# Four edits to a tuned attention-and-FFN gradient kernel: the last forward blocks turned by TensorE and the FFN's inputs loaded first, a gate product placed behind the evictions, the row-norm gradient partly on ACT, the tail's packing pinned

## The chip, the cores and the metric

The kernel runs on one core of one Trainium2 chip. The metric is device time in microseconds (us) from the first to the last instruction of the core, some 1.7 us more than the span that the profile shows. The executions of one kernel mostly lie within 0.7% of each other, so I quote medians and, for comparisons, the ratio of fast runs with its 95% interval. All runs of this study were in the fast state; single fast runs reached 3169 us before and 3139 us in some of the variants.

Some words: TensorE writes its products to PSUM banks, and an eviction is the copy by which VectorE (DVE) or ScalarE (ACT) takes a result out of such a bank and frees it. GpSimd (Pool) and SyncE (SP) issue the transfers here. A hole is a stretch in which TensorE stands still. The granted clock is the share of its full clock that TensorE got, and the DMA share is the mean busy share of the 16 DMA engines.

## The reference, cut to what matters

```python
# 2048 tokens of width 448; 16 heads of 256; segments of 32 tokens behind 8 memory rows (64 segments)
for s in range(n_seg):                       # the memory makes this loop sequential
    h = concat([mem, xs]);  q, k, v = h @ Wq, h @ Wk, h @ Wv
    o = (softmax(mask(q @ k.T * scale)) @ v) @ Wo
    mem = o[:, :M];  outs.append(o[:, M:])
h  = x + A(layernorm(x))                     # A is the loop above
h2 = h + (silu(n @ w_gate) * (n @ w_up)) @ w_down,   n = layernorm(h)
# returned: h2 and, by jax.vjp, the gradients of x, mem0, Wq, Wk, Wv, Wo, w_gate, w_up, w_down
```

So there are four stages: a forward chain of 64 dependent segments, the FFN forward and backward (8 passes of 256 tokens), a backward chain of 64 dependent segments, and a tail in which the weight gradients are large matrix products over stored blocks.

## The kernel before

Only the places that the change touches are shown. W, A and B are regions of on-chip memory, dr[...] are scratch tensors in DRAM; `tc.issue_after(x)` places an instruction behind `x` in the order of its own engine.

The gradient of the row norm, nearly all on DVE (32 calls: 16 in the FFN, 16 in the backward chain):

```python
def ln_bwd(k, outs, dxn_ap, xn_ap, rstd_col, t1, junk):
    nc.vector.reduce_sum(out=m1[:], in_=dxn_ap, axis=AX.X)
    nc.vector.tensor_tensor_reduce(out=junk, in0=dxn_ap, in1=xn_ap, ..., accum_out=m2[:])
    # ... m1s = m1 / D, m2s = -m2 / D on 128x1
    nc.vector.tensor_scalar(out=t1, in0=dxn_ap, scalar1=m1s[:], scalar2=None, op0=ALU.subtract)
    nc.vector.scalar_tensor_tensor(out=t1, in0=xn_ap, scalar=m2s[:], in1=t1, op0=ALU.mult, op1=ALU.add)
    for out_ap, resid_ap, c0, c1 in outs:
        nc.vector.scalar_tensor_tensor(out=out_ap, in0=t1[:, c0:c1], scalar=rstd_col, in1=resid_ap, op0=ALU.mult, op1=ALU.add)
```

The end of the forward chain: the last blocks are turned to token-major order by DMA transposes on SP, behind the FFN's weight loads (`k.fl.at(...)`):

```python
        if jm == 15:
            # ... projection of the memory rows (32 matmuls into px)
            if end:
                at = k.fl.at(3).ins              # the last weight loads
        if jm == 15:
            for hf in range(2):
                to_token_major(mblk, NT + s // 16, hf, at)   # DMA transpose, then a store to X_o
            # ... memory rows: another DMA transpose, a store to XN
        # ...
        if end:
            for hf in range(2):
                to_token_major(xblk, t, hf, at)
```

An FFN pass (gates, ups, then the chain of products for the backward half):

```python
        def up(ps, fs):
            nc.scalar.copy(out=u[:, :, fs, :], in_=ps)
            nc.vector.tensor_tensor(out=z[:, :, fs, :], in0=ps, in1=g[:, :, fs, :], op=ALU.mult)
        # ...
        proj(Wg_sb, hnT, gate)
        nc.gpsimd.tensor_scalar(out=t1, in0=sg, scalar1=-1.0, scalar2=1.0, op0=ALU.mult, op1=ALU.add)
        proj(Wu_sb, hnT, up)
        to_v = nc.vector.tensor_tensor(out=t1, in0=g, in1=t1, op=ALU.mult)    # waits for Pool
```

The tail packs memory rows (M_v and so on) and turns them on TensorE between weight gradients:

```python
            def pack(ld=ld_b[g % 2], pk=pk_b[g % 2]):
                with tc.issue_after(k.last_om.ins):
                    nc.vector.tensor_copy(out=pk[:, 0:8], in_=...)
                nc.scalar.copy(out=pk[:, 8:16], in_=...)
            def turn(x_t, pk=pk_b[g % 2]):
                # ... 16 transposes on TensorE, two evictions
```

Of the kernel before, what the change touches and what calls it, by code (L numbers as in the profile page):

```python
# [247 lines left out]
def ln_bwd(k, outs, dxn_ap, xn_ap, rstd_col, t1, junk):  # L248

    nc, smal, D = k.nc, k._small, k.D  # L250
    m1 = smal.tile([P, 1], FP32, name="lnb_m1")
    nc.vector.reduce_sum(out=m1[:], in_=dxn_ap, axis=AX.X)
    m2 = smal.tile([P, 1], FP32, name="lnb_m2")
    nc.vector.tensor_tensor_reduce(out=junk, in0=dxn_ap, in1=xn_ap, scale=1.0, scalar=0.0,
                                   op0=ALU.mult, op1=ALU.add, accum_out=m2[:])
    m1s = smal.tile([P, 1], FP32, name="lnb_m1s")
    nc.vector.tensor_scalar(out=m1s[:], in0=m1[:], scalar1=1.0 / D, scalar2=None, op0=ALU.mult)
    m2s = smal.tile([P, 1], FP32, name="lnb_m2s")
    nc.vector.tensor_scalar(out=m2s[:], in0=m2[:], scalar1=-1.0 / D, scalar2=None, op0=ALU.mult)
    nc.vector.tensor_scalar(out=t1, in0=dxn_ap, scalar1=m1s[:], scalar2=None, op0=ALU.subtract)  # L260
    nc.vector.scalar_tensor_tensor(out=t1, in0=xn_ap, scalar=m2s[:], in1=t1, op0=ALU.mult, op1=ALU.add)
    for out_ap, resid_ap, c0, c1 in outs:
        nc.vector.scalar_tensor_tensor(out=out_ap, in0=t1[:, c0:c1], scalar=rstd_col, in1=resid_ap, op0=ALU.mult, op1=ALU.add)


class _FFNLoads:
# [31 lines left out]
    def at(self, place):  # L298
        k, sync = self.k, self.k.nc.sync
        if place == 0:  # L300
            self.rows(self.Wg_sb, k.aps["B_w_gate"])
            self.rows(self.Wu_sb, k.aps["B_w_up"])
        elif place == 1:
            self.load_in(0, 0)
            self.load_in(1, 1)
        elif place == 2:
            self.turned_rows(self.WdT_sb, k.dr["Td"])
            sync.dma_start(out=self.Wd_sb, in_=k.aps["B_w_down"].rearrange("(c p) d -> p c d", p=P))
        else:
            sync.dma_start(out=self.WgT_sb, in_=k.dr["Tg"])  # L310
            return sync.dma_start(out=self.WuT_sb, in_=k.dr["Tu"])
# [47 lines left out]
def forward_chain(k: _K):  # L359
# [193 lines left out]
    def to_token_major(blk, t, hf, ins=None):  # L553
        ot = stg()
        with tc.issue_after(ins) if ins is not None else nullcontext():
            nc.sync.dma_start_transpose(out=ot.rearrange("p (a b) -> p a b", b=P),
                                        in_=blk[:, 16 * hf:16 * hf + 16, :].rearrange("p c n -> p (c n)"))
        save((dr["X_o"][t][:, hf * 2048:(hf + 1) * 2048], ot))
# [42 lines left out]
    for s in range(NSEG):  # L601
# [9 lines left out]
        with k.prio.crit():  # L611
# [85 lines left out]
            if end:  # L697
                k.fl.at(0)
                k.fl.at(1)
# [13 lines left out]
            if end:  # L713
                k.fl.at(2)
# [46 lines left out]
        if r == 2:  # L761
            w = bu // 4
# [3 lines left out]
        at = None  # L766
        if jm == 15:
# [6 lines left out]
            if end:  # L774
                at = k.fl.at(3).ins
        if jm == 15:
            for hf in range(2):
                to_token_major(mblk, NT + s // 16, hf, at)
# [3 lines left out]
            r0 = (NT + s // 16) * P  # L782
# [3 lines left out]
        if end:  # L786
            for hf in range(2):
                to_token_major(xblk, t, hf, at)
# [7 lines left out]
def ffn_phase(k: _K, back):  # L796
# [36 lines left out]
    nc.gpsimd.dma_start(out=hc[:, 0:24, :], in_=xn[:, 8:32, :])  # L833
    nc.gpsimd.dma_start(out=hc[:, 24:32, :], in_=dr["XN"][S:, :].rearrange("(s m) d -> s m d", m=8))
    nc.gpsimd.dma_start(out=dr["HC"][S:, :].rearrange("(s m) d -> s m d", m=8), in_=xn[:, 0:8, :])
# [78 lines left out]
    for n, gi in enumerate(turns):  # L914
# [21 lines left out]
        def up(ps, fs):  # L936
            nc.scalar.copy(out=u[:, :, fs, :], in_=ps)
            nc.vector.tensor_tensor(out=z[:, :, fs, :], in0=ps, in1=g[:, :, fs, :], op=ALU.mult)
# [4 lines left out]
        nc.gpsimd.tensor_scalar(out=t1, in0=sg, scalar1=-1.0, scalar2=1.0, op0=ALU.mult, op1=ALU.add)  # L943
        proj(Wu_sb, hnT, up)
        to_v = nc.vector.tensor_tensor(out=t1, in0=g, in1=t1, op=ALU.mult)
# [61 lines left out]
def backward_chain(k: _K):  # L1007
# [38 lines left out]
    def load_seg(s):  # L1046
# [9 lines left out]
        nc.gpsimd.dma_start(out=P_sb.rearrange("p h n -> p (h n)"), in_=dr["P_all"][s])  # L1056
# [206 lines left out]
def tail_phase(k: _K):  # L1263
# [26 lines left out]

    def load_x(nm, hf):
# [11 lines left out]
    def load_m(nm, hf):  # L1303
        todo = []
        for g in range(NG):
# [4 lines left out]
            def pack(ld=ld_b[g % 2], pk=pk_b[g % 2]):  # L1310
                with tc.issue_after(k.last_om.ins):
                    nc.vector.tensor_copy(out=pk[:, 0:8], in_=ld[:, :, 0:8, :].rearrange("p s c m -> p c s m"))
                nc.scalar.copy(out=pk[:, 8:16], in_=ld[:, :, 8:16, :].rearrange("p s c m -> p c s m"))

            def turn(x_t, pk=pk_b[g % 2]):
                for q in range(2):
                    pt = k.ph1()
                    for i in range(8):
                        nc.tensor.transpose(pt[:, i * P:(i + 1) * P], pk[:, 8 * q + i].rearrange("p s m -> p (s m)"), ident[:, :])
# [10 lines left out]
    def d_by_e(lhs_of, rhs_of, nblk, widths, store, at=None):  # L1330

        pa = accs(7)
        for b0 in range(0, nblk, 4):
# [8 lines left out]
            for b in range(b0, min(nblk, b0 + 4)):  # L1342
                for g in range(2):
                    w = widths[g]
                    nc.tensor.matmul(pa[6][64 * g:64 * g + 64, 0:w], lhsT=lhs_of(b)[:, (KC - 1) * P:D], rhs=rhs_of(b, g),  # L1345
                                     start=(b == 0), stop=(b == nblk - 1), skip_group_check=True)
        for i in range(6):
            kc, g = divmod(i, 2)
            res = resbuf()
            k.evac(res[:, 0:widths[g]], pa[i][:, 0:widths[g]])  # L1350
            store(kc, g, res[:, 0:widths[g]])
        res = resbuf()
        for g in range(2):
            k.evac(res[64 * g:64 * g + 64, 0:widths[g]], pa[6][64 * g:64 * g + 64, 0:widths[g]])
            store(KC - 1, g, res[64 * g:64 * g + 64, 0:widths[g]])

    def rows_by_d(lhs_of, rhs_of, nblk, n, store):
        pa = accs(n)
        for bi, b in enumerate(nblk):
            for i in range(n):  # L1360
                nc.tensor.matmul(pa[i][:, 0:D], lhsT=lhs_of(b, i), rhs=rhs_of(b), start=(bi == 0), stop=(bi == len(nblk) - 1))  # L1361
        for i in range(n):
            res = resbuf()
            k.evac(res[:, 0:D], pa[i][:, 0:D])
# [116 lines left out]
```

## Time and profile before

| | us |
|---|---|
| median of 4 runs | 3152.92 (3142.21 to 3165.51) |
| profiled run, span and granted clock | 3151.8, 0.982 |
| forward chain, to its last DVE operation on the memory | 1051.6 |
| seam, from there to the first FFN projection | 14.0 |
| FFN, to the first matmul of the backward chain | 334.5 |
| from there to the score-gradient product of segment 63 | 5.9 |
| backward chain, that product of segment 63 to that of segment 0 | 1041.7 |
| tail, from there to the end | 704.1 |

I cut every profile of this study into the same stages by the start times of the same instructions, so a gain can be told by stage. The page and the waits for the first three stages stand in the prediction below. Two lines that it tells but does not show are TensorE's waits in the tail, from the view of waits (engine, tile and line, releaser: total us, times, longest):

```profile
PE ph L1319 <- DVE arA L1312: 13.3, 1, 13.3
PE psf L1361 <- DMA arA<-in_grad_out_dram: 4.5, 1, 4.5
```

L1319 is the first transpose of the packed memory rows; it stands ahead of the first weight gradient and waits for a packing copy.

### The profile page before, as it was taken

How to read it: one execution, taken by the hardware profiler on the slowest of the kernel's cores; microseconds unless marked ns; L12 is line 12 of the kernel's file. 1: busy time of each engine (PE TensorE's matmuls, PEld its weight loads, DVE VectorE, ACT ScalarE, POOL GpSimd, SP SyncE). 2: the span in 40 equal slices, each digit the busy share in tenths (PEclk: the TensorE clock that was granted, in tenths of full speed). 3: DMA queues.
4: the chain of work that ended last, by engine and by line, in shares of the span. 5: the costliest groups of instructions: out<-in, count | busy, mean ns of one | idle time of the engine just before them, and what ended most of it. 6: DMA issues, size and time to landing. Idle time of an engine off the chain costs nothing.

```text
span 3151.8 us, 108174 instructions
## 1 busy us (share of the span) xinstructions
PE 2920.1 (93%) x47572; PEld 1737.8 (55%) x47582; DVE 1360.2 (43%) x3441; ACT 1069.0 (34%) x2533; POOL 671.9 (21%) x1515
## 2 busy tenths in 40 slices
PE   6999999999988869999999999999999899999998
PEld 3555555555544445556666666666666454444443
DVE  4555455455455557664454444454444201111110
ACT  2444344344444424333333333433334101111210
POOL 2222222222222222231112112122111111211111
PEclk9999999999999989999999999999999899999999
DMA  6666666656755987794545545555545899969941
GB/s 239 174 174 173 168 172 171 180 161 170 194 164 164 263 215 188 186 320 121 139 132 142 142 128 140 141 134 148 130 139 132 272 283 245 189 183 201 186 151 56
DMA packets 747947, 552.33 MB, mean 175 GB/s; under 512 B 608916, under 2 KB 643716, under 8 KB 745044
## 3 DMA queue, kind: packets, MB, share of 16 engines
q1 hardware_dynamic: 695668, 389.32, 50.8%
q0 software_dynamic: 51808, 156.09, 14.9%
q8 instruction: 373, 6.11, 0.8%
q14 instruction: 98, 0.80, 0.1%
HBM read 168.01 MB, written 234.23 MB: 128 GB/s over the span
## 4 chain that ended last, share of the span: by engine, by line
PE 72%; issue 7%; DVE 7%; DMA 7%; ACT 3%; POOL 2%; SPq 1%; ACTq 0%; POOLq 0%; DVEq 0%
PE psf L1340 8%; PE po L1174 7%; PE psf L1125 6%; PE psf L535 5%; PE psf L646 5%; PE po L691 4%; PE psf L1361 4%; PE psf L1102 4%; PE fx L1238 3%; PE psf L868 3%; PE fx L464 2%; DVE arA L75 2%; PE fx L1345 2%; PE psf L549 2%; PE psf L1196 2%
## 5 line engine op out<-in xcount | busy, mean ns | idle before, releaser
L75 DVE CAST arA<-psf 128x256 bf16<-128x256 f32 (+3 forms) x933 | 427.0, 480 | 799.5 <-PE psf L1340 258.9
L76 ACT CAST arA<-psf 128x96 bf16<-128x96 f32 (+5 forms) x915 | 352.4, 409 | 1048.1 <-PE psf L1340 256.5
L1174 PE MATMUL po<-arW,arA 128*32 128x448 bf16 x6144 | 346.2, 354 | 5.0 <-DMA arW<-Tq 3.3
L1340 PE MATMUL psf<-arW,arA 128*128 128x512 bf16 x980 | 246.9, 379 | 0.0
L1125 PEld LDWEIGHTS <-arW 128*128 128x128 bf16 x8192 | 214.8, 96 | 27.7 <-issue 27.7
L1340 PEld LDWEIGHTS <-arA 128*128 128x128 bf16 x1440 | 136.0, 98 | 165.0 <-issue 13.7
L1125 PE MATMUL psf<-arA,arW 128*128 128x40 bf16 x8192 | 218.5, 180 | 8.6 <-DVE arA L1200 5.1
L646 PE MATMUL psf<-arW,arA 128*64 128x512 bf16 x1536 | 219.3, 386 | 0.0
L1174 PEld LDWEIGHTS <-arA 128*32 128x32 bf16 x6144 | 151.6, 96 | 115.3 <-ACT arA L76 9.3
L535 PE MATMUL psf<-arW,arA 128*32 128x512 bf16 x3072 | 191.8, 382 | 12.6 <-DVE arA L733 12.6
L868 PE MATMUL psf<-arW 128*128 128x256 bf16 (+1 forms) x1288 | 154.2, 282 | 36.2 <-DVE arA L934 19.2
L76 ACT CAST arB<-psf 128x64 bf16<-128x64 f32 (+3 forms) x384 | 121.8, 318 | 151.1 <-PE psf L539 106.6
L868 PEld LDWEIGHTS <-arW 128*128 128x128 bf16 (+1 forms) x1344 | 105.6, 99 | 91.4 <-issue 78.0
L691 PE MATMUL po<-arW,arA 128*32 128x256 bf16 (+1 forms) x4096 | 145.9, 269 | 9.7 <-DVE arA L75 7.5
L1135 ACT COPY arA<-psf 128x1024 bf16<-128x1024 bf16 x128 | 123.4, 1015 | 4.1 <-PE psf L1134 2.2
L1102 PEld LDWEIGHTS <-arW 128*128 128x128 bf16 x2048 | 86.4, 99 | 62.7 <-issue 58.9
L535 PEld LDWEIGHTS <-arA 128*32 128x32 bf16 x3072 | 70.2, 96 | 89.0 <-DVE arA L733 18.2
L691 PEld LDWEIGHTS <-arA 128*32 128x32 bf16 x4096 | 96.9, 98 | 32.3 <-DVE arA L75 10.8
L464 PE MATMUL fx<-arA,arW 128*128 128x64 bf16 (+1 forms) x2048 | 84.1, 195 | 32.5 <-ACT arB L76 19.3
L76 ACT COPY arA<-psf 128x512 bf16<-128x512 bf16 (+2 forms) x138 | 80.3, 582 | 92.8 <-DVE arA L75 90.7
L1102 PE MATMUL psf<-arB,arW 128*128 128x80 bf16 x2048 | 96.8, 201 | 14.4 <-DVE arB L1155 4.3
L464 PEld LDWEIGHTS <-arW 128*128 128x128 bf16 (+1 forms) x2048 | 70.6, 98 | 54.8 <-issue 32.5
(283 smaller groups left out, 4606.6 us busy)
## 6 DMA issues: line engine op xcount, KB each, us to landing
arW<-T SPq DMA_DIRECT2D x256, 128.0 KB
X_o<-arA SPq DMA_DIRECT2D x33, 512.0 KB
T<-arA SPq DMA_DIRECT2D x64, 256.0 KB
X_v<-arA POOLq DMA_DIRECT2D x32, 512.0 KB, 6.5
X_k<-arA POOLq DMA_DIRECT2D x32, 512.0 KB, 3.9
X_q<-arA POOLq DMA_DIRECT2D x32, 512.0 KB, 3.3
out_dram<-arA POOLq DMA_DIRECT2D x90, 128.0 KB, 3.9
VG<-arA SPq DMA_DIRECT2D x64, 160.0 KB
```

The lines of the kernel that those rows point to most:

```text
L75: return nc.vector.tensor_copy(out=out, in_=in_)
L76: return nc.scalar.copy(out=out, in_=in_)
L464: nc.tensor.matmul(banks[w][:, i * 64:(i + 1) * 64], lhsT=lhsT, rhs=xr[lo:hi, kc, :], start=(kc == 0 and i == 0), stop=(kc == KC - 1), ski ...
L535: nc.tensor.matmul(banks[w][32 * q:32 * q + 32, :], lhsT=hT_roll[:, kc, sl, M:L], rhs=(Wq_sb, Wk_sb)[w][:, kc, col(q, b)], start=(kc == 0) ...
L646: nc.tensor.matmul(pV[b][64 * g:64 * g + 64, 0:512], lhsT=hT_flat[:, kc, sl * L:sl * L + 64], rhs=Wv_sb[:, kc, n * 512:(n + 1) * 512], sta ...
L691: nc.tensor.matmul(pO[32 * q:32 * q + 32, 0:w], lhsT=xblk[:, j, r * SEG:(r + 1) * SEG], rhs=Wo_sb[:, cj(j), 256 * dh:256 * dh + w], start= ...
L868: nc.tensor.matmul(ps[fp][:, f2 * 256:(f2 + 1) * 256], lhsT=Wt[lo:hi, kc, c * P:(c + 1) * P], rhs=xT[lo:hi, kc, :], start=(kc == 0 and f2 ...
L1102: nc.tensor.matmul(ps[b][:, i * 2 * L:(i + 1) * 2 * L], lhsT=lhs[:, at, :], rhs=rhs_bd[:, cl // 2, :, :].rearrange("p g n -> p (g n)"), st ...
L1125: nc.tensor.matmul(pss[b][:, jj * L:(jj + 1) * L], lhsT=WoT_sb[:, kc, c * P:(c + 1) * P], rhs=do_roll[:, kc, sl, :], start=(kc == 0), stop ...
L1174: nc.tensor.matmul(pH[32 * (j % 4):32 * (j % 4) + 32, 0:D], lhsT=blk[nm][:, j, r * SEG:(r + 1) * SEG], rhs=WT[:, cj(j), :], start=(nm == " ...
L1340: nc.tensor.matmul(pa[2 * kc + g][:, 0:w], lhsT=lhs_of(b)[:, kc * P:(kc + 1) * P], rhs=rhs_of(b, g), start=(b == 0), stop=(b == nblk - 1), ...
L1361: nc.tensor.matmul(pa[i][:, 0:D], lhsT=lhs_of(b, i), rhs=rhs_of(b), start=(bi == 0), stop=(bi == len(nblk) - 1))
```

## The change

Its intent, in the author's four parts, split as I use them below:

1. **Seam**: TensorE turns the last blocks (68 transposes) in place of five DMA transposes; h and grad_out are loaded ahead of the weights; the copies of rows to HC move from the start of the FFN to passes 3 and 4; a load of P_all leaves Pool's line; one earlier DMA transpose (T0k of the last group of segments) moves from segment 62 to 59.
2. **Product**: the product that waits for Pool is placed behind the evictions of the up projection.
3. **Norm**: two of the row-norm gradient's passes go from DVE to ACT.
4. **Tail**: packing and turning are pinned behind the first weight gradient.

```diff
-    nc.vector.reduce_sum(out=m1[:], in_=dxn_ap, axis=AX.X)
+    nc.scalar.activation(out=t1, in_=dxn_ap, func=ACT.Copy, accum_out=m1[:])
...
-    nc.vector.tensor_scalar(out=t1, in0=dxn_ap, scalar1=m1s[:], scalar2=None, op0=ALU.subtract)
-    nc.vector.scalar_tensor_tensor(out=t1, in0=xn_ap, scalar=m2s[:], in1=t1, op0=ALU.mult, op1=ALU.add)
+    nc.vector.scalar_tensor_tensor(out=t1, in0=xn_ap, scalar=m2s[:], in1=dxn_ap, op0=ALU.mult, op1=ALU.add)
+    nc.scalar.activation(out=t1, in_=t1, func=ACT.Identity, scale=rstd_col, bias=m1s[:])
     for out_ap, resid_ap, c0, c1 in outs:
-        nc.vector.scalar_tensor_tensor(out=out_ap, in0=t1[:, c0:c1], scalar=rstd_col, in1=resid_ap, op0=ALU.mult, op1=ALU.add)
+        nc.vector.tensor_tensor(out=out_ap, in0=t1[:, c0:c1], in1=resid_ap, op=ALU.add)
... (FFN loads: load_in(0, 0) now first, load_in(1, 1) last)
+    def turned_by_pe(blk, halves):
+        for q in range(4):
+            pt = k.ps1()[:].bitcast(BF16)
+            for i in range(8):
+                nc.tensor.transpose(pt[:, i * P:(i + 1) * P], blk[:, 8 * q + i, :], ident[:, :])
+            k.evac(halves[q // 2][:, (q % 2) * 1024:(q % 2 + 1) * 1024], pt, "vs"[q % 2])
...
-        if r == 2:
-            w = bu // 4
+        if bu == 2 or bu == (3 if bm == NSEG // 8 - 1 else 6):
+            w = int(bu > 2)
...
+        if end:
+            last_x = [stg(), stg()]
+            turned_by_pe(xblk, last_x)
... (the same for mblk and the memory rows, then four plain stores to X_o behind the weight loads)
-        if end:
-            for hf in range(2):
-                to_token_major(xblk, t, hf, at)
...
-    nc.gpsimd.dma_start(out=hc[:, 0:24, :], in_=xn[:, 8:32, :])
-    ... (two more copies to HC)
+    def rows_of_contexts(i):
+        with tc.issue_after(k.pool_op.ins):
+            ... (the same three copies, called in passes 3 and 4)
...
-            nc.vector.tensor_tensor(out=z[:, :, fs, :], in0=ps, in1=g[:, :, fs, :], op=ALU.mult)
+            k.last_up = nc.vector.tensor_tensor(out=z[:, :, fs, :], in0=ps, in1=g[:, :, fs, :], op=ALU.mult)
...
-        to_v = nc.vector.tensor_tensor(out=t1, in0=g, in1=t1, op=ALU.mult)
+        with tc.issue_after(k.last_up.ins):
+            to_v = nc.vector.tensor_tensor(out=t1, in0=g, in1=t1, op=ALU.mult)
...
-        nc.gpsimd.dma_start(out=P_sb.rearrange("p h n -> p (h n)"), in_=dr["P_all"][s])
+        with tc.issue_after(k.pool_op.ins) if s == NSEG - 1 else nullcontext():
+            nc.gpsimd.dma_start(out=P_sb.rearrange("p h n -> p (h n)"), in_=dr["P_all"][s])
...
             def pack(ld=ld_b[g % 2], pk=pk_b[g % 2]):
-                with tc.issue_after(k.last_om.ins):
+                with tc.issue_after(k.last_ev["v"].ins):
                     nc.vector.tensor_copy(...)
-                nc.scalar.copy(...)
+                with tc.issue_after(k.last_ev["s"].ins):
+                    nc.scalar.copy(...)
... (turn: each transpose placed behind the last matmul of the gradient before it)
```

## The prediction

> **What bounds the kernel now.** The page's first part, then the busy tenths and the table of windows, split the span into four stages: the forward chain (to 1051 us), the FFN forward and backward (1066 to 1400), the backward chain (to 2463) and the tail of weight gradients (to 3152).
>
> ```profile
> PE 2920.1 (93%) x47572; PEld 1737.8 (55%) x47582; DVE 1360.2 (43%) x3441; ACT 1069.0 (34%) x2533; POOL 671.9 (21%) x1515
> 1102.80:1126.60 23.80, 4.63 (x41) 3.11 (x40) 4.04 (x10) 3.23 (x6) 3.76 (x7) 0.67 1.06 256
> 1160.40:1203.50 43.10, 37.67 (x269) 22.62 (x268) 29.42 (x51) 17.38 (x30) 11.22 (x17) 0.92 0.75 177
> 1241.70:1279.30 37.60, 35.75 (x270) 21.88 (x269) 27.43 (x44) 14.63 (x27) 7.97 (x11) 1.00 0.77 193
> ```
>
> TensorE is the bound (93%; DVE 43%, ACT 34%). A change gains only where TensorE stands still, so I looked for the holes. The second row is the start of FFN pass 1: 4.63 us of matmuls in 23.8, clock 0.67, DMA share 1.06 (saturated). The third and fourth rows are passes 2 and 4: the same 269 or 270 matmuls take 43.1 and 37.6 us. TensorE's waits in the FFN, in the view of waits, come down to two, and the timeline of TensorE shows what follows:
>
> ```profile
> PE psf L868 <- DVE arA L934: 19.2, 1, 19.2
> PE psf L868 <- DVE arA L938: 16.3, 7, 5.4
> 1178.52 8.28 PE L868 MATMUL psf<-arW 128*128 128x256 bf16 x56 [5.43 <-DVE arA L938]
> 1218.60 6.36 PE L868 MATMUL psf<-arW 128*128 128x256 bf16 x56 [2.09 <-DVE arA L938]
> 1335.32 7.93 PE L868 MATMUL psf<-arW 128*128 128x256 bf16 x56 [3.65 <-DVE arA L938]
> ```
>
> After a hole of 3.65 or 5.43 us the next 56 matmuls also run slower (7.93, 8.28 us against 6.36). The chain that ended last tells where the 19.2 us come from, and where TensorE stands still at the two seams:
>
> ```profile
> 1048.54 6.23 issue
> 1055.80 7.92 PE fx L770 x32
> ...
> 1112.05 7.29 DMA arA<-arA
> 1120.64 5.04 DMA DH<-dh_t
> ...
> 2466.42 9.24 DMA arA<-M_v
> 2475.74 0.44 DVE arA L1312
> 2476.22 0.29 PE ph L1319
> ```
>
> Seam one: TensorE is idle 4.7 us before L770, because Pool holds a load of P_all (L1056, needed only 350 us later) in front of the small copy L752 that L770 needs. Pass 1's gates write over the stage buffers that the last DMA transposes (L556) still read; those sit behind each other on the sync queue and end near 1119. Seam two: DVE and ACT stand at the packing copies (L1312, L1313) from 2460 and 2464 on for a load of M_v, and TensorE behind them for 13.3 us.
>
> **What the Trainium skill says.** "TensorE: Matmul & The Clock Gate", What's actually happening: about 3.4 us of idleness halves the clock until some 3.4 us of work. The trace agrees in kind (6.36 against 7.93 and 8.28 us); a 2.41 us hole before 1294.35 was enough too. Same page, PE-mode transpose: a transpose was measured at about 275 ns. This trace decides otherwise for batches: 54 at L843 took 3.18 us, 59 ns each, and 16 at L909 took 1.06 us, 66 ns. "DMA: Bandwidth & Descriptors", DMA Transpose (X-bar), Constraints: a plain DMA transpose can be issued from SP or ACT only. In the trace all are on SP, in line with the loads, and L764 held that line 11.97 us. "ScalarE: Activation LUTs", What ACT_TABLE_LOAD costs: an ACTIVATE costs 186 ns plus 0.833 ns per element, and 93 ns more per pointer operand. For 448 elements that gives 0.56 us plain and 0.75 us with scale and bias. The trace has plain copies of 128x448 at 0.53 to 0.57 us.
>
> **The change, part by part.** I also read the order of instructions of both builds. TensorE's, DVE's and ACT's are the same up to the end of the forward chain's last segment, so nothing moves in the first 1050 us but an early Pool copy to HC, where TensorE waits for no such copy.
>
> (1) Seam one. The P_all load leaves Pool's line: 4.7 us of idleness go. In come 64 transposes of the last two blocks and 4 of the memory rows: 68 x 62 ns = 4.2 us of TensorE, with nine PSUM evictions at 0.69 (DVE) and 1.0 us (ACT). In the new order the evictions of one staging half come only after pass 0's seven gates, because that buffer still waits for its own store; two of five PSUM banks stay held, which I put at 1 us. h and grad_out now come ahead of most weights: before, DVE waited for h until 1057.7, but TensorE had L770 to do until 1063.7, so this is hidden. Sum: about 0.
>
> (2) The hole of 19.2 us. Five DMA transposes of blocks and rows, and L764, leave the sync queue near the FFN's weights, and a part of the HC copies leaves this stretch. Pass 1's gates now wait for four plain X_o stores (2 MB). Bytes issued from 1040 to those stores: about 11 MB of weights, 0.5 of h and grad_out, 1.5 of T1, VG and Tv, 2 of X_o, 15 MB; at the 279 to 285 GB/s that the windows show here that is 53 us, so about 1093. The gates start near 1103. So I expect the hole to close: 19.2 us, plus the slow restart (128 matmuls in 17.07 us against 14.5 at 113 ns): 2.6 us.
>
> (3) The seven holes of 16.3 us. DVE ran the product L945, which waits for Pool's L943, in front of four or five of the evictions L938. The new order has it after the last of the seven in every pass. Gone: 16.3 us, and the slow restarts at 1178, 1294 and 1335: 1.9 + 1.6 + 1.6 = 5.1 us. Pool's lateness itself (it waits for grad_out, 2.58 us) stays, now behind 11.7 us of TensorE work: 56 matmuls of L868 (6.4) and 28 of L963 (5.3). DVE needs 2.0 + 2.0 + 3 x 1.05 = 7.1 us there, so it fits if Pool is less than some 4 us late.
>
> (2) and (3) together: 19.2 + 2.6 + 16.3 + 5.1 = 43.2 us at most. The HC copies (2.5 MB) now come in passes 3 and 4: 5 and 4 us of a full DMA in passes of 36 us at a share of 0.8, so late loads there are likely. I take 7 us off: **36 us**.
>
> (4) The row-norm gradient. For each of 32 tiles DVE loses a reduction (0.62) and a subtraction (0.68), and its last operations turn into plain adds; ACT gains two passes, 0.56 + 0.75. DVE sheds some 40 us in all, but TensorE waits for it nowhere in these places: in the backward chain the segment after a norm has its first DVE eviction 0.2 us late and TensorE does not stop. DVE's sum of products now also waits for ACT's pass where they share a buffer. The new order has ACT's two passes between evictions in which ACT waited 1.2 and 1.6 us for TensorE, so they fit. **1 us.**
>
> (5) The tail. Packing and turning are pinned behind the first weight gradient; the 13.3 us of TensorE go, and a slow restart (120 matmuls in 24.7 us against 22.7): 15 us at most. But the X_o blocks that this gradient reads are issued by SP until 2484, each waiting for an earlier one to land, at a DMA share of 0.92 to 0.98, and a part of its other operand (L349) until 2490. If TensorE starts at 2467 it catches up with them: block 16 of 20 would be due at 2467 + 16 x 1.14 = 2485 and lands near 2491. So about 7 us are given back. **8 us.** From 2505 to 3092 TensorE is busy 99 to 100%: nothing to gain. The last 60 us (15 us idle, a load of grad_out that needs HC's place) are untouched.
>
> Sum: 0 + 36 + 1 + 8 = 45 us: 3158.8 - 45 = **3114 us**.
>
> **Rivals.** (a) A new wait takes the hole's place: the X_o stores stand behind all weights in the same queue, and if the DMA reaches them at 1115 instead of 1093, 12 us come back. For it: the DMA share was 1.08. Against it: the transposes and HC copies that made it so are gone. Time: about 3126. (b) The FFN becomes bound by DMA or by the Pool-DVE-ACT chain: 30.8 us of DMA per pass (0.8 x 38.5) in 36, and ACT's second norm pass stands between gates. A quarter of the gain would go: about 3125. (c) All holes close and the tail isn't paced by loads: 43 + 15 + 5 = 63 us: 3096. Against it: the DMA shares above. (d) The extra evictions and the held PSUM banks at seam one cost more than the wait they replace, 5 us or so: 3119.
>
> **Range and chances.** Three runs before spread from 3142 to 3166, so 12 us either way for the median. With (a) and (b) together I come to 3138, with (c) to 3096: range **3093 to 3138**. Faster by over 2% needs 63 us, which is (c) in full: **0.15**. Slower by over 2% needs a new stall of 100 us: **0.02**. Within 2%: **0.83**.
>
> **What would show it.** TensorE's waits for the up evictions (L938 before) should be near 0, and passes 2 to 6 take 36 to 37 us each at a clock near 1.0. No hole over 5 us at the start of pass 1; if it is there, its releaser is a store of X_o. TensorE's first FFN projection starts within 2 us of 1065.6. The backward chain still takes 16.04 us a segment and 16.9 after a norm. The tail's first gradient starts near 2467 on the old clock but shows small DMA waits. The prediction is wrong if the X_o stores end after 1110, if HC copies stall passes 3 and 4 by more than 5 us each, or if the backward chain's segments change.

## The result, and the profile after

The changed kernel took 3108.39 us (median of 4 runs, 3105.46 to 3112.69), the kernel before 3152.92. The ratio is 0.9858 with a 95% interval of 0.9816 to 0.9901. A ratio here is the mean time of one kernel's fast runs over that of the other's in the same rounds, so it is not quite the ratio of the medians. The gain is 44.5 us, 1.4%: within 2%, as predicted, and 5.6 us below the predicted 3114. The prediction started from 3158.8 us, the median of the three runs that it had.

| stage, us | before | after | difference |
|---|---|---|---|
| forward chain | 1051.6 | 1052.5 | +0.9 |
| seam | 14.0 | 12.4 | -1.6 |
| FFN | 334.5 | 293.5 | -41.0 |
| to segment 63 | 5.9 | 7.3 | +1.4 |
| backward chain | 1041.7 | 1034.0 | -7.7 |
| tail | 704.1 | 704.0 | -0.1 |

The busy times on the page of the changed kernel:

```profile
PE 2914.8 (94%) x47640; PEld 1735.5 (56%) x47650; DVE 1331.6 (43%) x3381; ACT 1112.6 (36%) x2634; POOL 674.7 (22%) x1511
```

Its table of windows for passes 1 to 4 (stretch, its length, then busy time with instructions of TensorE, weight loads, DVE, ACT and Pool, the granted clock, the DMA share and GB/s):

```profile
1101.80:1138.90 37.10, 35.43 (x268) 21.56 (x266) 27.05 (x46) 16.92 (x33) 11.22 (x17) 1.00 0.93 237
1138.90:1175.00 36.10, 36.10 (x272) 22.03 (x271) 26.95 (x47) 18.50 (x35) 10.32 (x15) 1.00 0.86 197
1175.00:1211.00 36.00, 36.00 (x270) 21.81 (x269) 25.40 (x40) 18.17 (x34) 8.45 (x12) 1.00 0.97 219
1211.00:1247.50 36.50, 35.66 (x269) 21.70 (x268) 25.34 (x40) 16.92 (x33) 8.96 (x13) 1.00 0.97 240
```

TensorE is as busy as before in total; it only stands still less. Pass 1, which began with 23.8 us of near standstill and took 57.6 us (1102.8 to 1160.4), is now a pass like the others, at a clock of 1.00. Passes 3 and 4, which carry the HC copies, have a DMA share of 0.97 and are hardly longer. TensorE's waits in the FFN of the changed kernel:

```profile
PE fx L1014 <- DVE arW L990: 2.5, 2, 1.7
...
PE psf L890 <- DVE arA L956: 0.7, 2, 0.4
```

And TensorE's timeline there (start, us, line, operation, tiles, shape, count; an idle time before it would stand in brackets):

```profile
1101.88 18.97 PE L890 MATMUL psf<-arW 128*128 128x256 bf16 x168
...
1139.40 18.97 PE L890 MATMUL psf<-arW 128*128 128x256 bf16 x168
...
1175.10 19.28 PE L890 MATMUL psf<-arW 128*128 128x256 bf16 x168
```

The waits of 19.2 and 16.3 us for DVE's evictions are gone. The 112 gate and up matmuls of a pass and the 56 of the data gradient behind them, which were two groups with a hole between them, run as one group of 168 in 18.97 us, 113 ns each. Pool's lateness itself stays, as predicted, but only DVE sees it now: the view of the product's line says what DVE waited for ahead of it (us, times), here before:

```profile
  POOL arW L943: 15.7, 6
```

And in the changed kernel:

```profile
  POOL arW L965: 9.5, 4
```

At the seam, TensorE's timeline of the changed kernel shows the new transposes (L557, L790) around the projection that used to wait 4.68 us for Pool:

```profile
1051.90 1.96 PE L557 MATMUL psf<-ident,arA 128*128 128x128 bf16 x32
1053.69 6.22 PE L778 MATMUL fx<-arW,arA 128*128 128x448 bf16 x32
1059.75 2.08 PE L557 MATMUL psf<-ident,arA 128*128 128x128 bf16 x32
1061.96 0.38 PE L790 MATMUL psf<-ident,arB 128*128 128x128 bf16 x4
```

The tail is the surprise. TensorE's waits there in the changed kernel:

```profile
PE psf L1396 <- DMA arW<-X_o: 13.0, 1, 13.0
PE psf L1396 <- DMA arA<-in_grad_out_dram: 3.3, 1, 3.3
```

And the chain of waits ahead of its first weight gradient (start, us, what):

```profile
2417.27 13.43 DMA arW<-X_o
2430.74 2.05 PE psf L1396 x5
```

The 13.3 us wait for a packing copy has turned into a 13.0 us wait for the first X_o load. The first matmul of the first weight gradient comes 31.0 us after segment 0's product, against 31.9 before, where the whole of 15 us at most was to be gained. The backward chain is 7.7 us shorter, which no step of the prediction had.

### The profile page after: what moved, and what is told of

Same layout as the page of the kernel before. It is cut to its first block, busy times and chain, and to the rows that moved or that the text cites. A ratio compares the mean times of both kernels' runs of the same rounds, so it can differ in the third digit from the quotient of the medians.

```text
span 3103.7 us, 108341 instructions
## 1 busy us (share of the span) xinstructions
PE 2914.8 (94%) x47640; PEld 1735.5 (56%) x47650; DVE 1331.6 (43%) x3381; ACT 1112.6 (36%) x2634; POOL 674.7 (22%) x1511
## 4 chain that ended last, share of the span: by engine, by line
PE 72%; issue 11%; DVE 6%; DMA 5%; ACT 4%; POOL 2%; SPq 1%; ACTq 0%; POOLq 0%; DVEq 0%
PE po L1200 7%; PE psf L1151 7%; PE psf L535 6%; PE psf L652 5%; PE po L697 4%; PE psf L1375 4%; PE psf L890 4%; PE psf L1128 4%; PE psf L1396 4%; PE fx L1264 3%; PE fx L1014 3%; PE fx L464 2%; PE psf L1222 2%; DVE arA L75 2%; PE psf L549 2%
## 5 line engine op out<-in xcount | busy, mean ns | idle before, releaser
L75 DVE CAST arA<-psf 128x256 bf16<-128x256 f32 (+3 forms) x933 | 427.2, 480 | 808.6 <-PE psf L1375 275.2
L535 PE MATMUL psf<-arW,arA 128*32 128x512 bf16 x3072 | 193.8, 385 | 12.5 <-DVE arA L738 12.5
L890 PE MATMUL psf<-arW 128*128 128x256 bf16 (+1 forms) x1288 | 146.3, 274 | 1.3 <-DVE arA L956 0.7
L890 PEld LDWEIGHTS <-arW 128*128 128x128 bf16 (+1 forms) x1344 | 102.4, 97 | 51.4 <-issue 40.8
L76 ACT COPY arA<-psf 128x512 bf16<-128x512 bf16 (+3 forms) x142 | 84.3, 594 | 99.9 <-DVE arA L75 90.3
L464 PE MATMUL fx<-arA,arW 128*128 128x64 bf16 (+1 forms) x2048 | 84.3, 196 | 32.4 <-ACT arB L76 19.2
L1436 POOL DMA_DIRECT2D out_dram<-arA x96 | 51.7, 546 | 249.7 <-DVE arA L75 246.9
```

Of the source, the lines that this page charges most:

```text
L75: return nc.vector.tensor_copy(out=out, in_=in_)
L76: return nc.scalar.copy(out=out, in_=in_)
L464: nc.tensor.matmul(banks[w][:, i * 64:(i + 1) * 64], lhsT=lhsT, rhs=xr[lo:hi, kc, :], start=(kc == 0 and i == 0), stop=(kc == KC - 1), ski ...
L535: nc.tensor.matmul(banks[w][32 * q:32 * q + 32, :], lhsT=hT_roll[:, kc, sl, M:L], rhs=(Wq_sb, Wk_sb)[w][:, kc, col(q, b)], start=(kc == 0) ...
L890: nc.tensor.matmul(ps[fp][:, f2 * 256:(f2 + 1) * 256], lhsT=Wt[lo:hi, kc, c * P:(c + 1) * P], rhs=xT[lo:hi, kc, :], start=(kc == 0 and f2 ...
```

## The experiments

Three questions were open. Which part brought the 41 us of the FFN, and do the parts add up? Did the norm on ACT shorten the backward chain? Why did the tail gain nothing? My theory for the three: product and seam bring the FFN's gain and nearly add up; the backward chain's 7.7 us are chance; the tail is paced by the X_o loads. The rivals: the norm has a share in both chains, and the packing pin works but something else in the changed kernel takes its gain back.

### 1. Each part alone on the kernel before (one call, 3 rounds each)

**The product alone** (before, plus `k.last_up = ...` in `up` and):

```diff
-        to_v = nc.vector.tensor_tensor(out=t1, in0=g, in1=t1, op=ALU.mult)
+        with tc.issue_after(k.last_up.ins):
+            to_v = nc.vector.tensor_tensor(out=t1, in0=g, in1=t1, op=ALU.mult)
```

> The kernel before with part (3) alone: the gate product g*t1 is placed behind the last up eviction of its pass. Theory A (the seven holes of 16.3 us and their slow restarts of 5.1 us are this one misplaced product): waits of TensorE for the up evictions fall from 16.3 us to under 2 us, FFN stage (first gate matmul to first matmul of the backward chain, 334.5 us before) falls by 19 to 22 us, while the 19.2 us hole at the start of pass 1 stays. Rival (the holes come from Pool and DMA being late, so they only move on to the next place that needs the product): FFN stage falls by less than 8 us and TensorE's waits move to the matmuls of the data gradient. Whole time about 3132 under A, about 3147 under the rival.

Measured: 3134.37 us (3131.47 to 3138.2), ratio to before 0.9925 [0.9901, 0.9949]. The FFN took 313.0 us, 21.5 less. TensorE's waits in the FFN:

```profile
PE psf L868 <- DVE arA L934: 19.3, 1, 19.3
```

The hole of pass 1 is as before, and the waits for the up evictions are gone from the list; they have not moved to another place either. Passes 2 to 5 started at 1168.98, 1204.67, 1240.68 and 1276.38, so they take 35.7 to 36.0 us each. One reordered DVE instruction per pass is half of the whole gain, and 21.5 is what the prediction's part (3) says (16.3 + 5.1 = 21.4).

**The norm alone** (before, with `ln_bwd` of the changed kernel):

> The kernel before with part (4) alone: the row-norm gradient partly on ACT. Between the two profiles the backward chain (first product of segment 63 to that of segment 0) fell from 1041.7 to 1034.0 us. Theory A (the norm is not the cause; the 7.7 us are mostly single late segments that differ from run to run): segments after a norm fall by 0.07 us each (16.92 to 16.85), about 1 us in all, and the sum of the late segments stays a matter of chance; FFN within 1 us of 334.5. Rival (the norm on DVE held up the evictions): the backward chain again takes about 1034 us with the same few late segments as the changed kernel. Whole time within 3 us of before under A, 8 us less under the rival.

Measured: 3149.23 us (3147.85 to 3154.92), ratio 0.9975 [0.9951, 0.9999]. The segments after a norm took 16.86 us in the median against 16.91, so the chain gains 16 x 0.05 = 0.8 us. The backward chain as a whole was 1035.7 us here, but it was 1035.7 with the product alone too, where nothing in it differs from before. The FFN was 329.4 us, 5.1 less than before. I had not expected this; the waits for the up evictions were 13.7 instead of 16.3 us and pass 1's hole 18.4 instead of 19.2. With a single profile, and a spread of 5.0 us among FFNs of equal instructions (below), it may be chance. The interval of the times just excludes 1, though, so whether the norm alone gains a few us stays open.

What the moved passes cost, by groups of instructions (busy us, mean ns, then the idle time before them) in the backward chain of the kernel before:

```profile
L260 DVE TENSOR_SCALAR t<-fx,lnb_m1s 128x448 f32<-128x448 f32 x15 | 10.2, 680 | 0.0
...
L252 DVE TENSOR_REDUCE lnb_m<-fx 128x1 f32<-128x448 f32 x16 | 10.0, 625 | 18.6 <-PE fx L1253 18.6
```

And in that of the changed kernel:

```profile
L261 ACT ACTIVATE t<-t,lnb_m1s,rstd 128x448 f32<-128x448 f32 x16 | 12.2, 761 | 20.9 <-DVE t L260 19.7
...
L252 ACT ACTIVATE t<-fx 128x448 f32<-128x448 f32 x16 | 9.0, 562 | 0.7 <-PE fx L1279 0.7
```

DVE loses 0.62 and 0.68 us a call and ACT gains 0.56 and 0.76, as the prediction's estimate had it, and 0.21 more for a read of the accumulator, which it had not. TensorE waits for neither.

**The tail alone** (before, with `tail_phase` of the changed kernel):

> The kernel before with part (5) alone: packing and turning in the tail pinned. In the changed kernel the 13.3 us wait for the packing was followed by a 13.0 us wait for the first X_o block, and the tail took 704.0 against 704.1 us. Theory A (the DMA engines are full from the end of the backward chain on, so the wait only changes its name): the tail takes 703 to 705 us, the wait for packing is gone and one of 11 to 14 us for X_o is there. Rival (the wait for X_o comes from another part of the change, such as the shifted loads): the tail falls to 695 to 697 us. Whole time the same as before under A, 8 us less under the rival.

Measured: 3148.73 us (3145.47 to 3153.76), ratio 0.9971 [0.9947, 0.9996]. The tail took 696.3 us, 7.8 less than before; the prediction had 8 for it. TensorE's first wait in it:

```profile
PE psf L1370 <- DMA arW<-X_o: 7.1, 1, 7.1
```

So the pin does what it was meant to do on its own, and the X_o loads hold TensorE for 7.1 us, not 13. The wait stands in front of the first block (first matmul at 2472.51), and no later block waits. The rival held: in the changed kernel something else makes these loads land later.

**The seam alone** (the changed kernel with the norm, the tail and the place of the product as before):

> The kernel before with parts (1) and (2) alone: last blocks turned by TensorE, h and grad_out ahead of weights, HC copies and P_all load later; norm, product and tail as before. Theory A (parts add up): the 19.2 us hole at pass 1 is gone, FFN stage falls from 334.5 by 20 to 23 us, the holes for the up evictions stay at 14 to 18 us; the seam itself (end of the last output projection to the first gate matmul) stays within 2 us of 14.4 us. Rival (holes hide each other): with pass 1 unblocked the up-eviction holes grow, FFN falls by less than 15 us. Whole time about 3130 under A, above 3137 under the rival.

Measured: 3135.79 us (3132.14 to 3136.92), ratio 0.9925 [0.9898, 0.9952]. The seam took 12.5 us, 1.5 less, but the FFN 325.6: only 8.9 less, although the hole of pass 1 is closed. TensorE's waits in the FFN:

```profile
PE psf L890 <- DVE arA L960: 24.5, 8, 6.7
```

The 56 data-gradient matmuls of pass 1, behind the up evictions, in TensorE's timeline:

```profile
1123.17 8.50 PE L890 MATMUL psf<-arW 128*128 128x256 bf16 x56 [6.65 <-DVE arA L960]
```

The waits for the up evictions grew from 16.3 to 24.5 us: pass 1 now has one too (6.65 us, with a slow restart). Closing one hole lets TensorE run into the next wait earlier: the rival held. Alone, product, seam and norm gain 21.5 + 8.9 + 5.1 = 35.5 us in the FFN; together they gain 41.0. They are not independent: the product's new place takes away the wait into which the seam's gain ran. And the tail of this kernel, with the old packing, shows that the seam part is enough to hold the X_o loads back: its first X_o load was issued 17.2 us after the first of the DCt loads ahead of it in SP's line, as in the changed kernel (17.0), against 12.4 before and 12.1 with the tail alone. Over all profiles it is 11.3 to 13.5 us in the four without the seam part and 15.0 to 17.8 in the nine with it and an unchanged order of these loads.

### 2. The changed kernel again, and parts taken out of it (one call, 3 rounds each)

**Unchanged, once more:**

> The changed kernel once more, unchanged. Theory S (systematic): the late start of the X_o loads follows from the order in which Pool's transfers were issued, so the tail is again 703 to 705.5 us and TensorE again waits 12 to 14 us for the first X_o block. Theory C (chance): the loads landed late only in that profile, and the tail comes out near 696 (the value of the tail part alone), the time near 3101. On the backward chain: if its 1034 us are chance it may come out anywhere from 1033 to 1042; if the seam part causes it, within 1033 to 1036.

Measured: 3109.37 us (3105.83 to 3112.01), ratio 0.986 [0.984, 0.9879]. Tail 704.1 us with a wait of 13.0 us for X_o: the same as before to 0.1 us, so the late loads are systematic. The backward chain, however, was 1039.5 instead of 1034.0 us with the same instructions, and the forward chain 1047.6 instead of 1052.5.

**With the tail of the kernel before:**

> The changed kernel with the tail's packing and turning in the order of before. Theory S (in the combination the pin gains nothing, because TensorE only exchanges a wait for packing against a wait for X_o loads): tail 703 to 706 us, TensorE waits 15 to 18 us for a packing copy on DVE and little for X_o; ratio to the changed kernel within 0.1%, so about 3109. Rival (the pin is worth its 7.8 us here too): tail 711 to 713, time about 3117.

Measured: 3114.6 us (3111.64 to 3135.75), ratio 0.9892 [0.9854, 0.9929]. Tail 704.8 us. TensorE waits as before, and a little longer:

```profile
PE ph L1345 <- DVE arA L1338: 15.8, 1, 15.8
```

In this company the pin gains 0.7 us in the tail (704.8 against 704.1): with it TensorE waits for X_o, without it for the packing copy, until about the same time. The medians differ by 5 us, so the expected 0.1% was missed. In this profile 2 to 5 us of it lie in the FFN (298.5 us, with a wait of 4.3 us in pass 0), but the other three runs have no profile, so that the pin is worth a few us here is not ruled out.

**With the first M_v fetches placed behind the first weight gradient** (they read many small pieces just when the X_o loads are under way):

```diff
-    mems[0][0][0]()
+    with tc.issue_after(k.first_dwo.ins):
+        mems[0][0][0]()
```

> The changed kernel with the first two M_v fetches (many small pieces, on Pool's queue) held back until the first weight gradient's last matmul. Theory D (the DMA engines are full at this seam, and the M_v pieces take the bandwidth from the X_o loads): the first X_o block lands 6 to 9 us earlier, TensorE's wait for it falls from 13.0 to 4 to 7 us, tail 695 to 698, time about 3101. Rival E (the X_o loads are late because the loads of DCt before them on the same queue are late): wait for X_o stays 12 to 14 us, tail 702 to 705. Rival F (packing now comes too late): a new wait of 5 us or more for the packing or turning behind the first gradient, tail 704 or more.

Measured: 3112.98 us (3104.61 to 3119.1), ratio 0.987 [0.9842, 0.9899]. This run tested nothing. The edit ties a Pool transfer to a matmul, but `issue_after` only orders instructions of one engine, and the order of instructions turned out the same as in the changed kernel on every engine, wait for wait. I should have compared the orders before the run. It serves as a third profile of the changed kernel: FFN 294.1, backward chain 1043.2, tail 711.8 (with another 6.8 us wait of a TensorE transpose for an eviction, which came up at 4.7 us in one later run and at 2 us or less in the others), forward chain 1048.5. Three profiles of the same instructions thus span 9.2 us in the backward chain.

**With the DMA transposes of the last blocks** (`forward_chain` of the kernel before, which also puts the transpose of T0k back to segment 62; the new order of loads and all else as changed):

> The changed kernel with the last blocks of the forward chain turned by DMA transposes again, all else kept (h and grad_out first, row copies late, product last). Theory T (the transposes on the sync queue made the hole at the start of pass 1): TensorE waits 12 to 19 us at the start of pass 1, FFN 306 to 313 us, time 3121 to 3128; the seam is up to 5 us shorter or longer. Rival H (the row copies in this stretch made it): no hole over 5 us, FFN 292 to 297, time within 4 us of the changed kernel.

Measured: 3126.33 us (3118.55 to 3133.33), ratio 0.9906 [0.9881, 0.9931]. FFN 324.5 us. TensorE's timeline in pass 1:

```profile
1131.39 18.42 PE L872 MATMUL psf<-arW 128*128 128x256 bf16 x128 [23.12 <-DVE arA L938]
```

Two rows of SP's timeline ahead of it:

```profile
1054.32 19.22 SPq L763 DMA_TRANSPOSE arA<-arA  x1
...
1083.94 14.07 SPq L556 DMA_TRANSPOSE arA<-arA  x2
```

The hole is back, at 23.1 us. Followed back in the chain of waits it ends in the transposes and their stores: TensorE waits for DVE's gate evictions, those for the staging buffer, and that for a DMA transpose of 9.36 us and the X_o store behind it. Theory T held, and the FFN was even longer than its 306 to 313 (the profiled run was the slowest of the four, 3133.33 us). The first row above is the transpose of T0k, so this run does not tell its share from that of the last blocks. Nor are the 19.22 us the cost of a transpose alone: in the changed kernel a plain store in the same place, behind the same weight loads, held SP's line for 11.23 us. The seam was 8.0 us here: the loads' new order and the moved P_all load save 14.0 - 8.0 = 6.0 us, and turning on TensorE costs 12.4 - 8.0 = 4.4 of them.

### 3. The cause of the late X_o loads (one call, 3 rounds; then one more run)

The order of SP's and Pool's transfers at the start of the tail is the same in the changed kernel and with the tail alone, and so are their waits, but for one thing: each engine takes its eight completion semaphores in turn, and the changed kernel has this turn shifted, by four on Pool and by one on SP.

**The turn shifted back** (four transfers of 128 bytes on Pool and one on SP):

```diff
+    for i in range(4):
+        nc.gpsimd.dma_start(out=dr["scr"][i:i + 1, :], in_=ident[i:i + 1, 0:64])
+    nc.sync.dma_start(out=dr["scr"][4:5, :], in_=ident[4:5, 0:64])
     for tl in (Q_sb, K_sb, P_bd, dS_bd):        # the backward chain's setup
```

They are written at the start of the backward chain, but since they wait for nothing they were issued near the start of the program; so the turn is shifted in the forward chain as well. At the start of the tail, every transfer then has the same place in the turn as before.

> The changed kernel with four tiny transfers (128 bytes) on Pool and one on SP at the start of the backward chain, so that every later transfer takes the same one of the eight completion semaphores of its engine as in the kernel before (the changed kernel has them shifted by four and by one). Nothing else differs in the instruction streams. Theory L (the shifted turn of these semaphores is why the same loads of the tail land later in the changed kernel): the first X_o block lands as in the tail part alone, TensorE waits 6 to 9 us for it instead of 13, tail 695 to 698 us, time about 3101. Rival N (the turn does not matter, the loads are late for another reason, such as what else is on the DMA engines at that moment): wait 12 to 14 us, tail 703 to 706, time 3107 to 3111.

Measured: 3109.96 us (3108.53 to 3138.64), ratio 0.9884 [0.983, 0.9938]. Tail 703.0 us. TensorE's first wait in it:

```profile
PE psf L1401 <- DMA arW<-X_o: 13.1, 1, 13.1
```

Theory L fell. The turn of the semaphores is not the cause.

**M_v really later** (both fetches placed behind Pool's last store of the backward chain; the first was issued at 2438.17, 39 us after the first DCt load instead of 18):

```diff
-            nc.gpsimd.dma_start(out=OUT1[rows, :], in_=xn_t)
+            k.last_store = nc.gpsimd.dma_start(out=OUT1[rows, :], in_=xn_t)
...
-    mems[0][0][0]()
+    with tc.issue_after(k.last_store.ins):
+        mems[0][0][0]()
```

> What a_mem_late meant to do and did not: it left the instruction streams as they were, because that placement only orders instructions of one engine. Here the first two M_v fetches stand behind Pool's last store of the backward chain, so the first is issued about 21 us later (2440 instead of 2418). Theory D (the small pieces of M_v take the DMA engines from the X_o loads; 130 to 160 GB/s while both are under way): the first X_o block lands 5 to 7 us earlier, TensorE's wait for it falls from 13 to 6 to 8 us, tail 696 to 699, time about 3102. Rival E (the X_o loads are late by what comes before them): wait 12 to 14 us, tail 703 to 706. Rival F (packing comes too late): a new wait of 4 us or more behind the first weight gradient takes the gain back, tail 702 to 706.

Measured: 3108.35 us (3105.83 to 3112.78), ratio 0.985 [0.9826, 0.9875]. Tail 707.6 us, waits:

```profile
PE psf L1396 <- DMA arW<-X_o: 11.9, 1, 11.9
PE ph L1354 <- DVE arW L75: 4.7, 1, 4.7
```

The wait for X_o fell by 1.1 us only, so M_v is not what holds these loads back; theory D fell, rival E held, and with the second wait rival F as well. While they were in flight with no M_v fetch under way, the DMA engines moved 159 GB/s at a share of 1.01 (2420 to 2430), so the other transfers of that moment fill them without it.

**The HC copies back at the start of the FFN** (all else as changed):

> The changed kernel with the row copies to HC at the start of the FFN as before (2.5 MB), the last blocks still turned by TensorE. Theory T (the DMA transposes alone made the hole of pass 1, as the run that brought them back had 23.1 us of it): no hole over 5 us at the start of pass 1, FFN 292 to 298 us, time within 4 us of the changed kernel. Rival H (both are needed: the copies fill the DMA engines before the X_o stores that pass 1 waits for): a hole of 5 to 10 us, FFN 299 to 306, time 3113 to 3120.

Measured: 3116.98 us (3112.06 to 3119.44), ratio 0.9874 [0.985, 0.9899]. FFN 295.3 us, and pass 1 has no hole: theory T held for the FFN. Without the copies pass 3 took 36.0 us as with them, and pass 4 took 35.7; in the eight profiles that have them there, pass 4 took 36.3 to 37.0. Its tail had the X_o wait again, 12.8 us. Its time misses the expected 4 us to the changed kernel, by some 4 us more. The profile has them in the forward chain (1054.3), the backward chain (1041.1) and the tail (705.7), not in the FFN, and the forward and backward chains vary by as much among profiles of equal instructions. Whether the place of the HC copies costs anything outside of the FFN stays open.

**The first three X_o loads ahead of eight of the DCt loads** (only the four DCt loads ahead of them are needed for the first four blocks):

```diff
         for g in range(k.NB - NT):
             with k.tc.issue_after(k.last_load.ins):
                 sync.dma_start(out=self.DCt[:, NT + g], in_=dc8[g, :, 0:M])
+        self.outs(0, 3, 0, 6)
...
-    k.tl.outs(0, 7, 0, 6)
+    k.tl.outs(3, 7, 0, 6)
```

> The changed kernel with the first three X_o loads (the operands of the first weight gradient's first three blocks) issued on SP right behind the four DCt loads that these blocks need, ahead of the other eight DCt loads. Neither the shifted semaphores nor the M_v pieces explained the wait for X_o, so this asks whether it is only their place in SP's line. Theory Q (they wait in line behind DCt): TensorE's wait in front of the first gradient falls from 13 to 0 to 4 us, and a wait for a later load (DCt or the fourth X_o block) of 3 to 8 us comes up three blocks further on; tail 698 to 703, time 3102 to 3108. Rival B (the DMA engines are full, so what lands earlier here only makes the rest later by the same time): the waits still add up to 12 to 14 us, tail 703 to 706, time within 3 us of the changed kernel. Rival G (the whole wait goes): all waits under 5 us together, tail 692 to 697, about 3098.

Measured: 3108.56 us (6 runs, 3104.25 to 3139.45), ratio 0.9875 [0.9839, 0.9911]. Tail 699.7 us. TensorE's timeline:

```profile
2418.83 0.93 PE L1397 MATMUL psf<-arW 128*128 128x448 bf16 x4
...
2436.46 2.05 PE L1397 MATMUL psf<-arW,arA 128*128 128x448 bf16 x5 [12.49 <-DMA arA<-X_o]
```

The first weight gradient starts 15.2 us after segment 0's product instead of 31.0, without a wait. Three blocks later the whole wait stands there, 12.5 us long. The tail is 4.3 us shorter, about what three blocks take, so theory Q held for the tail and rival B for the sum of the waits. In the time of the whole kernel the gain does not show: 3108.56 against 3108.39 and 3109.37. So at this point TensorE is paced by the arrival of loads, and moving one load forward moves the wait back.

### What the experiments leave

| kernel | median us | FFN | backward chain | tail | first X_o wait or packing wait |
|---|---|---|---|---|---|
| before | 3152.92 | 334.5 | 1041.7 | 704.1 | 13.3 packing |
| product alone | 3134.37 | 313.0 | 1035.7 | 702.0 | 14.7 packing |
| norm alone | 3149.23 | 329.4 | 1035.7 | 701.8 | 14.6 packing |
| tail alone | 3148.73 | 335.1 | 1040.8 | 696.3 | 7.1 X_o |
| seam alone | 3135.79 | 325.6 | 1034.4 | 704.6 | 17.3 packing |
| changed | 3108.39 | 293.5 | 1034.0 | 704.0 | 13.0 X_o |
| changed, again | 3109.37 | 296.4 | 1039.5 | 704.1 | 13.0 X_o |
| changed, again (the run that tested nothing) | 3112.98 | 294.1 | 1043.2 | 711.8 | 12.8 X_o |
| old tail | 3114.60 | 298.5 | 1038.7 | 704.8 | 15.8 packing |
| DMA transposes back | 3126.33 | 324.5 | 1033.7 | 703.2 | 12.2 X_o |
| semaphores shifted back | 3109.96 | 295.0 | 1038.3 | 703.0 | 13.1 X_o |
| M_v later | 3108.35 | 296.3 | 1035.3 | 707.6 | 11.9 X_o |
| HC copies back | 3116.98 | 295.3 | 1041.1 | 705.7 | 12.8 X_o |
| X_o first | 3108.56 | 296.6 | 1040.1 | 699.7 | 12.5 X_o |

The norm did not shorten the backward chain by anything like 7.7 us: the four profiles with the norm on DVE have a mean of 1038.2 us, the ten with it on ACT 1038.0. The 7.7 us between the first two profiles are within the spread of equal instructions (1034.0 to 1043.2).

One thing stays unexplained. The forward and the backward chain together took 2091.6 to 2095.1 us in the four profiles without the seam part (mean 2092.9) and 2082.4 to 2095.4 in the ten with it (mean 2087.9). It fits that the seam alone gains 19 us by the medians of its call, but 10.4 in its seam and FFN. I compared these sums after the fact, and no run tests whether the seam part causes the 5 us.

What makes the X_o loads land later in every kernel that has the seam part's new order of loads is not settled. It is not the turn of the semaphores, not the M_v fetches, not the transposes on TensorE or the place of the HC copies (each taken out once, with the wait at 11.9 to 13.1 us throughout). What these kernels still share is the new order of the FFN's loads and the moved P_all load, 1000 us earlier, which I did not take out; and the value of the tail alone, 696.3 us, rests on one profile and four times.

## Why the prediction was right, point by point

The total was right (3108.4 in 3093 to 3138, within 2%), by two errors in its terms that nearly cancelled (the HC copies and the tail).

| step | predicted gain, us | measured |
|---|---|---|
| (1) seam | 0 (4.7 gone, 4.2 + 1 new) | 1.6 (6.0 gone, 4.4 new) |
| (2) hole of pass 1 | 21.8 | 20.1 (57.6 to 37.5 us) |
| (3) up evictions, passes 2 to 6 | 21.4 | 19.8 (199.6 to 179.8 us, HC copies included); 21.5 alone, over the FFN |
| HC copies in passes 3 and 4 | -7 | -0.6 to -1.3, in pass 4 |
| (2) + (3), the FFN | 36 | 41.0; 39.0 over seven profiles |
| (4) norm | 1 | below what the profiles resolve |
| (5) tail | 8 | 0.1 in the change, 7.8 alone |
| sum | 45 | 44.5 by the medians |

- **What bounds the kernel** was read rightly: TensorE's holes. Those that were named are where the gain came from.
- **(1)** TensorE gained more than the 4.7 us of waiting: the 32 matmuls behind that hole took 6.22 us instead of 7.92, a slow restart that the prediction left out. The banks that it saw held in pass 0 (1 us) show as well: that pass took 37.0 us in the mean of the four profiles without the seam part and 38.6 (36.9 to 43.6) in the nine that turn the blocks on TensorE, seven of which wait there for an eviction on L75. In the table this stands in the FFN.
- **(2)** The hole closed, by the mechanism named (the DMA transposes on the sync queue; bringing them back brought 23.1 us of it back, the HC copies alone none). The X_o stores were issued from 1072.7 to 1078.1 and pass 1's gates at 1101.9 met no wait, so rival (a) did not come.
- **(3)** held, and fairly exactly: 35.7 us in passes 2, 5 and 6, Pool's lateness left to DVE alone. What the prediction did not see is that (2) without (3) is worth only 8.9 us in the FFN.
- **The HC copies** are the mis-sized term in the FFN. "I take 7 us off" because passes with a full DMA might load late; they took 36.0 and 36.7 us against 35.7, at a DMA share of 0.97, and pass 3 takes 36.0 without the copies too. The mean of the FFN over the seven profiles that have its instructions as changed (293.5, 296.4, 294.1, 298.5, 295.0, 296.3, 296.6) is 295.8, a gain of 39.0 against the mean of the two that have them as before (334.5 and 335.1).
- **(4)** held: no TensorE wait, segments after a norm 16.86 us. DVE's busy time fell by 33.6 us with the norm alone (1360.2 to 1326.6), where some 40 were expected.
- **(5)** is the step that failed. The prediction let TensorE start on the first gradient at 2467 and catch up with the X_o loads near block 16 of 20, with about 7 us of waits and a gain of 8. That the first block would not be there was not seen. With the tail alone the whole wait, 7.1 us, stands in front of the first block, so the gain of 7.8 us met the 8 by luck and not by the catching up. In the changed kernel that wait is 13.0 us and nothing is gained. From its issue to the first matmul the first X_o load takes about as long in both (13.9 and 13.5 us); it is issued 11.2 us after segment 0's product with the tail alone and 17.6 us after it in the changed kernel. The prediction took the loads' times from the trace of before, where it is 11.5 us, and in every kernel with the seam part they came later, but for the run that moved them ahead. That a pin which removes a wait for packing only uncovers a wait for loads was in the text ("isn't paced by loads", rival (c)); its place and size were not.
- **Luck and the rest**: the gain of 45 us was met to 1 us although two terms were off by 6 and 8 us in opposite directions. By the stages' means over profiles the parts explain 39.0 + 1.6 = 41 us. The total itself is no accident of one call: the changed kernel, run again, gained 43.5 us by the medians. The 3 us between may be those of the two chains above, which no step of the prediction had.

No version beat the changed kernel beyond the spread of the runs.

## What to carry to other kernels

When an engine stands at an instruction that waits for a slow neighbour, while others behind it could run, move the instruction behind the evictions that the bound engine needs: here one reordered DVE product per pass was half of the gain, and the neighbour stayed as slow as it was. Before you count the worth of removing a wait, look up when the next operand of the released engine lands, in the trace of the combination and not of the part; here a packing wait of 13.3 us became a load wait of 13.0. And take two or three profiles of the same kernel before you explain a few us in a stage of 1000: equal instructions gave 1034.0, 1039.5 and 1043.2.

## What the Trainium skill lacked or had wrong

- "TensorE: Matmul & The Clock Gate", Part 4: PE-mode transpose and What's actually happening. The page gives about 390 ns for a transpose in isolation and 275 ns in one kernel; in batches this kernel's take 61 to 65 ns each, as a batch's time over its count (L557: 32 in 1.96 and 2.08 us). It has some 3.4 us of idleness ahead of the slow clock; here a hole of 2.26 us already gave 7.93 us for 56 matmuls (seam alone, at a granted clock of 0.50 from 1288.2 to 1291.6), while one of 2.46 us did not (6.36 us, norm alone), so the limit can lie well under 3.4 us and varies between holes.
- "ScalarE: Activation LUTs", What ACT_TABLE_LOAD costs, prices an ACTIVATE by its elements and pointer operands. One with an accumulator output is followed by a second instruction that the price leaves out, an accumulator read of 0.19 us behind each ACTIVATE of 0.54 us (16 of each in the FFN).
- None of the pages gives, for this chip, how long a transfer that is issued behind others holds SP's line for those after it. Here a DMA transpose held it for 11.97 us (before) and 19.22 us (DMA transposes back), and a plain store behind weight loads for 11.23 us (changed kernel, L747).
